# Softmax by products of ones on TensorE for batches 4 to 7, and other zero products ahead of the first chain

## The chip, the cores and the metric

The kernel runs on one core of one Trainium2 chip. The core has a matrix engine (TensorE, PE in the profile, its weight loads PEld), three engines for elementwise work (VectorE DVE, ScalarE ACT, GpSimd POOL), a queue engine (SyncE, SP), 16 DMA engines, an on-chip memory of 128 partitions and a matmul memory (PSUM) of eight banks. The metric is the device time in microseconds of one execution.

## The reference

Two parts stand behind each other. The first is a linear attention over 32 memory slots, for 8 batches, 8 heads, 576 tokens and a head size of 64; the second is a bilinear feed-forward layer over all 4608 tokens.

```python
a = np.exp(phi - max over tokens); a = a / (sum over tokens + 1e-9)
k_m = einsum('bhsm,bhsd->bhmd', a, k)
v_m = einsum('bhsm,bhsd->bhmd', a, v)
scores = q @ k_m^T / 8                       # 576 x 32 for each head
attn = softmax(scores, over the 32 slots)
x = (attn @ v_m), heads side by side         # 4608 x 512
out = ((x @ w_a) * (x @ w_b)) @ w_out        # d_ff is 1536
```

## The kernel before

Everything is done batch by batch, in 16-bit floats with 32-bit sums. The kernel never forms `attn @ v_m`: it folds the 32 memory values of each head into the weights (`fold`, tile `pva`, copied to `vab` by `take_fold`), so that the two wide products of a batch are `attn` against two folded weights of 256 x 1536.

The work of one batch is cut into named units, made by `units(b)`:

- `exp0 exp1`: exponentials of `phi` on ScalarE (L194). `qt0` to `qt3`: transposes of `q` on VectorE (L203).
- `kv`: sums of keys and values over tokens on TensorE (tile `pkv`, L212); `km` scales them on VectorE (tile `rep`). Then `rep` is transposed, either by TensorE and a VectorE copy (`kvt`, L241 and L242) or by a DMA transpose on SP's queue (`kvd`, L247).
- `sc`, or `s0` and `s1`: scores on TensorE for two groups of heads (tile `pscore`, four banks, L297). `e0`, `e1`: their exponentials on ScalarE (tile `E`, L310).
- the softmax division in one of two ways. One way: `den` multiplies `E` by a block matrix of ones on TensorE, so that each partition gets the sum of its head (tile `pD`, two products of 288 columns for each group, L320), and ScalarE takes the logarithm (`L`, L321); `nr` takes the exponential of the negated logarithm on ScalarE (`R`, L329) and multiplies `E` by it (`A`, L331), on VectorE for batches 0 to 2 and on GpSimd for batch 3. The other way, for batches 4 to 7: `ed` turns `E` by a DMA transpose so that tokens lie on partitions (L335), `sm0`, `sm1` sum 32 neighbours and take reciprocals on VectorE (L344, L345), `tn0` (GpSimd) and `tn1` (VectorE) multiply (L350), and `ad` turns the result back by another DMA transpose into `A` (L355).
- `v0 v1 v2`: folds of 512 columns each of both weights (16 products `pva`); `x0a` to `x2b` copy them out, one group on ScalarE and one on VectorE. For batches above 3 both groups of the middle fold (`x1`) are copied by ScalarE.

The wide products are `up_half` (L632): for a batch, one of 12 slices of d_ff and one half of the tokens, two products `pa` and two `pb`; ScalarE copies `pa` to `a_sb` (L640), VectorE multiplies it with `pb` into `ht` (L643). The last layer (`two_downs`, L504, tiles `py pv px`) takes two blocks of 128 tokens at a time with seven products where eight would be usual, over sums of `ht` that GpSimd forms (`sum_tokens`, tile `h_sums`, L486, four additions for a pair of blocks); sums of `w_out` are formed once by GpSimd (`sum_weights`). The first four blocks go through a plain product (`early_downs`, tile `po`, L429).

The order is written out by hand. Batches 0 and 1 start by `chain(...)`: a list of units, with `fN` for N zero products (`fill`, L151: 128 columns against a tile of zeros) and `yN` for N steps of `early_downs`. From batch 1 on, `ups(...)` runs the half steps of batch b, and after each one `work.advance()` hands out products of the last layer at a planned rate and then one entry (a slot) of the list for batch b+1 is called: `+` joins units in a slot, `'` names a unit of the batch after, `_` one of the batch before, `dN` pulls N products of the last layer, `L` calls `load` for two batches ahead, `-` is empty. Entries left over run behind the last half step. `second` serves batch 2 (units of 3 and 4), `every` batches 3 to 5, `last` batch 6. `work.settle()` ahead of scores and folds of later batches pulls products until a bank is given back. Eight PSUM banks are handed out in rotation by `banks`; a bank taken with `hold` stays out of it until it is freed.

Each engine works its own instructions in the order in which they were issued and waits where data or a buffer is not ready. `load(b)` issues four transfers on GpSimd's queue, behind whatever GpSimd was given before.

Of the kernel before, what the change touches and what calls it, by code (L numbers as in the profile page):

```python
# [18 lines left out]
def kernel(  # L19
# [127 lines left out]
    def fill(n, cols=512):  # L147

        pw = banks.tile([P, 512], F32, name="pw")
        for _ in range(n):  # L150
            nc.tensor.matmul(pw[:, :cols], warm[:, :P], warm[:, :cols], start=True, stop=True)  # L151

# [33 lines left out]
    def units(b):  # L186
# [136 lines left out]
        def normalise(g, hfs=slice(0, 2)):  # L323
# [6 lines left out]
            engine = nc.vector if b < 3 else nc.gpsimd  # L330
            engine.tensor_tensor(out=attn[b][:, g, sl], in0=t["E"][:, g, sl], in1=t["R", g][:, sl], op=ALU.mult)  # L331

        def e_turn():
            t["ET"] = mid.tile([P, 2, S], F16, name="E").rearrange("p g s -> p (g s)").rearrange("p (n x) -> p n x", x=P)
            nc.sync.dma_start_transpose(out=t["ET"], in_=t["E"].rearrange("p g s -> p (g s)"))  # L335

        def blocks(x):
            return t["ET"][:, slice(0, 5) if x == 0 else slice(5, 9)].rearrange("p n (j m) -> p (n j) m", m=M)

        def token_sums(x):  # L340
            if x == 0:
                t["sum"] = small.tile([P, 36], F32, name="sum")
            out = t["sum"][:, slice(0, 20) if x == 0 else slice(20, 36)]
            nc.vector.tensor_reduce(out=out, in_=blocks(x), axis=mybir.AxisListType.X, op=ALU.add)  # L344
            nc.vector.reciprocal(out=out, in_=out)  # L345

        def token_normalise(x):
            sums = t["sum"][:, slice(0, 20) if x == 0 else slice(20, 36)]
            engine = (nc.gpsimd, nc.vector)[x]
            engine.tensor_tensor(out=blocks(x), in0=blocks(x), in1=sums.unsqueeze(2).to_broadcast(list(blocks(x).shape)),  # L350
                                 op=ALU.mult)

        def a_turn():
            attn[b] = mid.tile([P, 2, S], F16, name="A")
            nc.sync.dma_start_transpose(out=attn[b].rearrange("p g s -> p (g s)").rearrange("p (n x) -> p n x", x=P),  # L355
                                        in_=t["ET"].rearrange("p n x -> p (n x)"))
# [20 lines left out]
        def take_fold(lo, hi, z):  # L377
            copies = (nc.scalar.copy, nc.scalar.copy if b > 3 and lo == 512 else nc.vector.tensor_copy)
            for g, engine_copy in enumerate(copies):
                pva, bank = t["pva", lo, z][g]  # L380
                engine_copy(out=vabs[b][z][:, g, lo:hi], in_=pva[:, 0:hi - lo])  # L381
                banks.free(bank)

        def one(f, *a):
            return lambda: f(*a)
# [30 lines left out]
        u["ed"] = e_turn  # L416
        for x in range(2):
            u[f"sm{x}"] = one(token_sums, x)
            u[f"tn{x}"] = one(token_normalise, x)
        u["ad"] = a_turn  # L420
# [248 lines left out]
    def half_steps(b, hf, lo=0):  # L669

        return [(b, i, (hf,)) for i in range(lo, NFF)]
# [50 lines left out]
    fill(64, P)  # L722
    chain(0, "exp0 exp1 f18 ks0 ks1 f4 kt0 qt0 qt1 f2 kt1 f4 qt2 qt3 f2 s0 e0 f2 den00 s1 e1 f8 den10 nr00 nr10 vs0 vs1 den01 den11 nr01 f4 vt0 vt1 hv0a nr11 hx0a f6 a0.0 a1.0 hv0b hx0b a0.1 a1.1 hv1a hx1a b0 b1 a3 hv1b a2 hx1b v1a x1a b2 b3 a4 a5 v1b x1b a6 a7 b4 b5 v2a x2a b6 b7 a8 a9 L v2b x2b a10 a11 b8 b9 b11 b10")
# [4 lines left out]
    ups(half_steps(1, 0, 4), slots(1, "- v2a+x2a+v2b+x2b - qt0' qt1'+exp0' exp1'+qt2' - kv'+km'+y9"))  # L728
    work.plan(S + HALF, 10)
    ups(half_steps(1, 1, 4), slots(2, "qt3 kvt - sc+e0+e1+den0+den1+nr0 - - L v0+nr1+x0b - - d4+v1+x0a+x1a+x1b d1"))  # L730
# [39 lines left out]
```

## Time and profile before

| | |
|---|---|
| times of three runs | 241.89, 241.90, 242.19 us |
| the profiled execution | 242.19 us, its span 240.5 us |
| TensorE busy | 228.8 us, 3070 products |
| VectorE busy | 170.4 us, 416 instructions |
| ScalarE busy | 153.4 us, 394 instructions |
| GpSimd busy | 152.4 us, 129 instructions |
| moved by DMA | 37.27 MB in 38436 packets |

The span runs from the first to the last instruction of the core; the time also holds what lies around it. A row of the profile names the line of the kernel, the engine, the operation, the tiles as out<-in, shapes, and either a count with busy time, mean duration and idle time ahead of it, or a start and a duration. An arrow names the instruction that ended a wait. Products on TensorE overlap, so that the distance from one start to the next, not the duration, is what a product takes of the engine's time; that distance is called the spacing below. Bank numbers and buffer numbers are left out of names.

### The profile page before, as it was taken

How to read it: one execution, taken by the hardware profiler on the slowest of the kernel's cores; microseconds unless marked ns; L12 is line 12 of the kernel's file. 1: busy time of each engine (PE TensorE's matmuls, PEld its weight loads, DVE VectorE, ACT ScalarE, POOL GpSimd, SP SyncE). 2: the span in 40 equal slices, each digit the busy share in tenths (PEclk: the TensorE clock that was granted, in tenths of full speed). 3: DMA queues.
4: the chain of work that ended last, by engine and by line, in shares of the span. 5: the costliest groups of instructions: out<-in, count | busy, mean ns of one | idle time of the engine just before them, and what ended most of it. 6: DMA issues, size and time to landing. Idle time of an engine off the chain costs nothing.

```text
span 240.5 us, 7733 instructions
## 1 busy us (share of the span) xinstructions
PE 228.8 (95%) x3070; PEld 168.4 (70%) x3070; DVE 170.4 (71%) x416; ACT 153.4 (64%) x394; POOL 152.4 (63%) x129
## 2 busy tenths in 40 slices
PE   7868999999987999999999999999999999999993
PEld 7634664456664877868777877868777778888882
DVE  4635784469949977979786777679776776656642
ACT  2266671669696579777778458776776777465330
POOL 7953244499999419593879699692929265946001
PEclk9999999999999999999999999999999999999999
DMA  6999999999989999044599748998332332032145
GB/s 234 236 197 207 206 257 207 253 211 279 224 229 209 226 227 222 19 96 92 133 222 237 106 97 181 211 185 120 61 91 51 88 79 60 12 80 64 40 107 142
DMA packets 38436, 37.27 MB, mean 155 GB/s; under 512 B 14688, under 2 KB 32480, under 8 KB 38400
## 3 DMA queue, kind: packets, MB, share of 16 engines
q0 software_dynamic: 19264, 23.14, 52.2%
q1 hardware_dynamic: 18624, 12.85, 24.4%
q10 hardware_dynamic: 512, 0.79, 1.0%
q8 instruction: 24, 0.39, 0.6%
q14 instruction: 12, 0.10, 0.1%
HBM read 42.47 MB, written 9.44 MB: 216 GB/s over the span
## 4 chain that ended last, share of the span: by engine, by line
PE 75%; DMA 16%; DVE 2%; POOL 2%; issue 1%; ACT 1%; DVEq 0%; POOLq 0%
PE pa L632 18%; PE py L504 17%; PE pb L632 17%; PE pv L504 9%; DMA phi_sb<-in_phi_dram 6%; DMA wo_sb<-in_moe_w_out_dram 5%; PE pva L368 5%; DMA wa_sb<-in_moe_w_a_dram 5%; PE px L504 4%; PE pkv L212 2%; PE po L429 2%; PE pscore L297 1%; DVE A L331 1%; ACT E L310 1%; POOL q_sb L90 0%
## 5 line engine op out<-in xcount | busy, mean ns | idle before, releaser
L643 DVE TENSOR_TENSOR ht<-a_sb,pb 128x288 f16<-128x288 f16 x168 | 71.9, 445 | 32.0 <-ACT a_sb L640 23.9
L632 PEld LDWEIGHTS <-vab 128*128 128x128 f16 x768 | 72.4, 98 | 24.0 <-issue 5.9
L640 ACT CAST a_sb<-pa 128x288 f16<-128x288 f32 x168 | 65.5, 411 | 30.9 <-PE pa L632 29.4
L632 PE MATMUL pb<-A,vab 128*128 128x288 f16 x384 | 75.0, 286 | 0.9 <-ACT vab L381 0.5
L632 PE MATMUL pa<-A,vab 128*128 128x288 f16 x384 | 75.7, 287 | 0.1
L486 POOL TENSOR_TENSOR h_sums<-ht 128x768 f16<-128x768 f16 x28 | 46.3, 1657 | 27.2 <-DVE ht L643 27.2
L504 PEld LDWEIGHTS <-h_sums 128*128 128x128 f16 x384 | 37.2, 98 | 7.7 <-issue 1.4
L381 ACT CAST vab<-pva 128x512 f16<-128x512 f32 (+1 forms) x60 | 32.0, 574 | 9.4 <-PE pva L368 9.3
L504 PEld LDWEIGHTS <-ht 128*128 128x128 f16 x288 | 27.9, 98 | 6.0 <-issue 0.9
L381 DVE CAST vab<-pva 128x512 f16<-128x512 f32 (+1 forms) x44 | 26.8, 635 | 5.4 <-PE pva L368 5.2
L504 PE MATMUL py<-w_sums,h_sums 128*128 128x256 f16 x192 | 30.6, 273 | 0.0
L486 POOL TENSOR_TENSOR h_sums<-h_sums,ht 128x768 f16<-128x768 f16 x14 | 23.1, 1653 | 1.0
L486 POOL TENSOR_TENSOR h_sums<-ht,h_sums 128x768 f16<-128x768 f16 x14 | 23.0, 1642 | 0.9
L310 ACT ACTIVATE E<-pscore 128x288 f16<-128x288 f32 x32 | 10.9, 416 | 9.3 <-PE pscore L297 9.1
L504 PE MATMUL py<-w_sums,ht 128*128 128x256 f16 x96 | 16.1, 273 | 0.1
L511 ACT ACTIVATE u<-py 128x256 f32<-128x256 f32 x32 | 12.3, 384 | 5.6 <-PE py L504 5.1
L504 PE MATMUL pv<-w_sums,h_sums 128*128 128x256 f16 x96 | 15.9, 273 | 0.0
L504 PE MATMUL py<-wo_sb,ht 128*128 128x256 f16 x96 | 15.9, 273 | 0.0
L504 PE MATMUL px<-wo_sb,ht 128*128 128x256 f16 x96 | 15.2, 273 | 0.0
L203 DVE STREAM_TRANSPOSE qT<-q_sb 128x288 f32<-128x288 f32 x32 | 14.6, 462 | 0.0
L194 ACT ACTIVATE exp_sb<-phi_sb 128x576 f16<-128x576 f32 x16 | 10.8, 689 | 5.4 <-DMA phi_sb<-in_phi_dram 5.4
L504 PE MATMUL pv<-wo_sb,h_sums 128*128 128x256 f16 x96 | 14.2, 273 | 0.0
(69 smaller groups left out, 265.5 us busy)
## 6 DMA issues: line engine op xcount, KB each, us to landing
out_dram<-o_sb SPq DMA_DIRECT2D x68, 128.0 KB, 2.5
phi_sb<-in_phi_dram POOLq DMA_DIRECT2D x8, 576.0 KB, 5.8
kv_sb<-in_v_dram POOLq DMA_DIRECT2D x7, 576.0 KB, 11.0
kv_sb<-in_k_dram POOLq DMA_DIRECT2D x7, 576.0 KB, 8.6
q_sb<-in_q_dram POOLq DMA_DIRECT2D x6, 576.0 KB, 13.8
wo_sb<-in_moe_w_out_dram POOLq DMA_DIRECT2D x6, 256.0 KB, 13.8
q_sb<-in_q_dram POOLq DMA_DIRECT2D x4, 288.0 KB, 9.9
wa_sb<-in_moe_w_a_dram POOLq DMA_DIRECT2D x2, 512.0 KB, 13.7
```

Of the source, the lines that this page charges most:

```text
L194: nc.scalar.activation(out=t["exp"][:, 2 * z:2 * z + 2, :, :], in_=phis[b][:, 2 * z:2 * z + 2, :].rearrange("p c (i m) -> p c i m", m=M), ...
L203: nc.vector.transpose(out=t["qT"][:, hp, :].bitcast(F32), in_=qs[b][:, hp, :].bitcast(F32))
L212: nc.tensor.matmul(t["pkv"][g][0][32 * j:32 * j + 32], t["exp"][64 * r:64 * r + 64, hp, i, :], kvs[b][64 * r:64 * r + 64, :, hp, D * i:D * ...
L310: nc.scalar.activation(out=Ev[:, g, :, z, :], in_=pss, func=AF.Exp, scale=1.0 / (8.0 * CS))
L368: nc.tensor.matmul(t["pva", lo, z][g][0][32 * j:32 * j + 32, 0:hi - lo], t["kvT"][64 * r:64 * r + 64, 4 + g, M * j:M * j + M], w_sbs[z][64 ...
L381: engine_copy(out=vabs[b][z][:, g, lo:hi], in_=pva[:, 0:hi - lo])
L486: engine.tensor_tensor(out=out, in0=in0, in1=in1, op=op)
L504: nc.tensor.matmul(po, lhs[:, i], rhs[:, i], start=first and i == 0, stop=i == KH - 1, skip_group_check=not first)
L511: nc.scalar.mul(out=x, in_=po, mul=scale)
L632: nc.tensor.matmul(ps, vabs[b][x][:, g, P * i:P * (i + 1)], attn[b][:, g, HALF * hf:HALF * (hf + 1)], start=(g == 0), stop=(g == 1))
L640: nc.scalar.copy(out=a_sbs[b, i, hf], in_=ps)
L643: nc.vector.tensor_tensor(out=ht[:, i, t0:t0 + HALF], in0=a_sbs.pop((b, i, hf)), in1=ps, op=ALU.mult)
```

## The change

In front of the first chain, 64 full zero products become 46 full ones, 48 products of a 64 x 32 tile of zeros with 64 columns at four positions of the array in turn, and 14 full ones. In the first chain there are fewer zero products: 32 in place of 50.

The second way of dividing is taken out: batches 4 to 7 use `den` and `nr` like the others. `nr` multiplies on VectorE for batches 0 and 1 only and on GpSimd from batch 2. The second group of every fold is copied by VectorE again. The lists of slots for batches 2 to 7 are written anew; with them, batch 4's keys and values are transposed by TensorE (`kvt'`) in place of a DMA, `load(4)` is called ahead of batch 2's half steps, and `L` stands later in the lists.

```diff
+    def fill_tiles(n):
+        pw = banks.tile([P, 64], F32, name="pw")
+        for x in range(n):
+            j = x % 4
+            nc.tensor.matmul(pw[32 * j:32 * j + 32], warm[0:64, 0:32], warm[0:64, 0:64],
+                             start=True, stop=True, tile_position=(0, 32 * j))
...
-            engine = nc.vector if b < 3 else nc.gpsimd
+            engine = nc.vector if b < 2 else nc.gpsimd
             engine.tensor_tensor(out=attn[b][:, g, sl], in0=t["E"][:, g, sl], in1=t["R", g][:, sl], op=ALU.mult)
-        def e_turn():
-        def blocks(x):
-        def token_sums(x):
-        def token_normalise(x):
-        def a_turn():
...
-            copies = (nc.scalar.copy, nc.scalar.copy if b > 3 and lo == 512 else nc.vector.tensor_copy)
-            for g, engine_copy in enumerate(copies):
+            for g, engine_copy in enumerate((nc.scalar.copy, nc.vector.tensor_copy)):
...
-    fill(64, P)
-    chain(0, "exp0 exp1 f18 ks0 ks1 f4 kt0 qt0 qt1 f2 kt1 f4 qt2 qt3 f2 s0 e0 f2 den00 s1 e1 f8 den10 nr00 nr10 vs0 vs1 den01 den11 nr01 f4 vt0 vt1 hv0a nr11 hx0a f6 a0.0 ...")
+    fill(46, P)
+    fill_tiles(48)
+    fill(14, P)
+    chain(0, "exp0 exp1 f8 ks0 ks1 f4 kt0 qt0 qt1 f2 kt1 f2 qt2 qt3 s0 e0 den00 s1 e1 den10 nr00 nr10 f4 vs0 vs1 den01 den11 nr01 f4 vt0 vt1 hv0a nr11 hx0a f6 a0.0 ...")
...
-    ups(half_steps(1, 0, 4), slots(1, "- v2a+x2a+v2b+x2b - qt0' qt1'+exp0' exp1'+qt2' - kv'+km'+y9"))
+    ups(half_steps(1, 0, 4), slots(1, "- v2a+x2a+v2b+x2b+qt0' - - qt1'+exp0' exp1'+qt2' - kv'+km'+y9"))
     work.plan(S + HALF, 10)
-    ups(half_steps(1, 1, 4), slots(2, "qt3 kvt - sc+e0+e1+den0+den1+nr0 - - L v0+nr1+x0b - - d4+v1+x0a+x1a+x1b d1"))
-    second = "v2_+d2+x2a_+x2b_+exp0 - exp1 - kv+km+d2 qt0 d4+qt1+kvt qt2 L+d1+qt3+sc+e0 - d2+v0+e1+x0a+x0b - den0+exp0'+d2 v1+nr0+x1a x1b+d10+exp1' - qt0' v2+x2a+x2b+kv' - den1+km0' km1'+kvd' nr1+qt1' qt2' qt3' - d6"
-    every = "exp0' sc+exp1'+e0+e1+v0+x0a+x0b+d3+ed - kv'+km0' km1' - sm0 sm1+tn0+kvd' - tn1+d2 d3 v1+qt0'+x1a+ad d3+L+x1b qt1' - qt2' - v2+x2a+x2b - qt3' - - - - -"
-    last = "sc e0+e1+ed - v0+x0b - - sm0 x0a+sm1+tn0 d2+v1+d3+x1b+tn1 - ad+d6 x1a - - - - v2+x2a - - - - - x2b"
+    ups(half_steps(1, 1, 4), slots(2, "qt3 kvt - sc+e0+e1 - den0+den1+nr0 - v0+nr1+x0a x0b - v1+x1b x1a"))
+    second = "v2_+d1+x2a_+exp0 x2b_ exp1 - kv+km+d2 qt0 d4+kvt+qt1 - qt2+qt3+sc+e0 - e1+v0+d2+x0a+x0b den0+d3 exp0' v1+nr0+x1a x1b+qt0' L+d5 den1 v2+x2a exp1'+qt1'+x2b - - qt2'+kv'+nr1+km' - - qt3'+kvt'+d5"
+    every = "- sc+e0 e1 den0 nr0+v0+x0a+x0b - - exp0' exp1' - v1+x1b+x1a+kv'+km0'+d3 - den1+km1' kvd'+qt0' - - nr1+qt1' v2+x2a+x2b - qt2' - qt3' - - L"
+    last = "sc+e0 d3 - e1 v0+x0b - - den1 - - den0+d1 x0a+v1+x1b x1a+nr0 - - - v2+x2a - nr1 - - - - x2b"
     for b in range(2, B):
+        if b == 2:
+            load(4)
```

## The prediction

> **What bounds the kernel now.** I read the page first (engines, slices), then the chain of waits for the first 50 us, then TensorE's instructions in order of time with the idle time before each, and last VectorE and GpSimd around the one place where TensorE idles.
>
> ```profile
> span 240.5 us, 7733 instructions
> PE 228.8 (95%) x3070; PEld 168.4 (70%) x3070; DVE 170.4 (71%) x416; ACT 153.4 (64%) x394; POOL 152.4 (63%) x129
> PE   7868999999987999999999999999999999999993
> PEclk9999999999999999999999999999999999999999
> ```
> TensorE is the bound almost everywhere; only the first four slices, two near 70 us and the last are not full, and the granted clock is full throughout.
>
> ```profile
> 33.90 12.86 DMA wo_sb<-in_moe_w_out_dram
> ...
> 46.80 0.59 PE po L429 x2
> ```
> This is the chain of waits. Up to 46.76 us it is made of GpSimd's transfer issues and landings alone; the fifth slice of `wo_sb` then releases TensorE, which had idled 0.35 us. So what becomes faster before 46.8 us only lengthens that wait, and what becomes slower by up to 0.35 us costs nothing.
>
> ```profile
> 65.70 0.65 PE L297 MATMUL pscore<-qT,kvT 32*32 32x288 f16 x32
> 66.95 0.41 PE L320 MATMUL pD<-E,ones 128*128 128x288 f16 x2 [0.61 <-ACT E L310]
> 67.56 0.41 PE L320 MATMUL pD<-E,ones 128*128 128x288 f16 x2 [0.20 <-ACT E L310]
> ...
> 74.21 0.41 PE L368 MATMUL pva<-wb_sb,kvT 64*32 64x512 f16 x7 [1.22 <-DVE vab L381]
> 74.55 0.28 PE L504 MATMUL pv<-wo_sb,h_sums 128*128 128x256 f16 x1
> 74.67 0.44 PE L632 MATMUL pa<-A,vab 128*128 128x288 f16 x2
> ```
> ```profile
> 69.31 0.46 DVE L331 TENSOR_TENSOR A<-E,R 128x576 f16<-128x576 f16 x1 [3.09 <-ACT R L329]
> ...
> 71.36 2.19 DVE L331 TENSOR_TENSOR A<-E,R 128x576 f16<-128x576 f16 x1
> ```
> ```profile
> 71.58 1.65 POOL L486 TENSOR_TENSOR h_sums<-ht 128x768 f16<-128x768 f16 x1
> ```
> TensorE, VectorE, GpSimd in order of time: batch 2's softmax. The sums of exponentials wait for the exponentials just issued, and the second multiply takes 2.19 us instead of 0.46, ending just after a GpSimd addition ends; four `vab` copies queue behind it, and TensorE waits for them.
>
> ```profile
> 80.00:100.00 20.00, 20.00 (x357) 15.25 (x337) 16.91 (x45) 15.67 (x42) 10.72 (x9) 1.00 0.88 184
> ...
> 200.00:220.00 20.00, 20.00 (x174) 16.80 (x172) 13.35 (x31) 11.83 (x32) 13.53 (x9) 1.00 0.13 29
> ```
> Stretches of 20 us (columns: length, busy of PE, its weight loads, DVE, ACT, POOL; clock, DMA share, GB/s). TensorE shows no idle time from 80 to 220 us, so each product added there lengthens the run by its spacing, unless it fills a hidden wait.
>
> **The change part by part.** *Products of ones for batches 4 to 7 (`den`, L320), 16 more.* Spacing from
> ```profile
> 89.52 0.41 PE L320 MATMUL pD<-E,ones 128*128 128x288 f16 x2
> 89.77 0.38 PE L504 MATMUL py<-w_sums,h_sums 128*128 128x256 f16 x2
> ```
> Two take 0.245 us (89.52 to 89.77, start to start), so 8 pairs cost 1.96 us, all in the full stretch. They come one to three slots after the exponentials they read, so no wait is added.
>
> *Batch 4's key/value transposes by TensorE (`kvt`) instead of by DMA (`kvd`):* six products; the same six of batch 3 start at 82.67 and their successor at 83.00: 0.33 us, plus a VectorE copy of 0.53 us. Scores follow two slots and some 2 us later, which covers the copy.
>
> *The other engines.* ScalarE gains 16 logarithms (four in 1.35 us: 5.4) and 8 exponentials of 0.71 (5.7) and gives 8 copies of 0.60 to VectorE (-4.8). VectorE loses the reductions (5.9), reciprocals (2.1) and multiplies (3.1) of the token path and batch 2's two multiplies (2.65), and gains those 8 copies at 0.68 (5.5). GpSimd loses four multiplies of 1.26 and gains ten of 1.28: +7.7, to 160 of 240 us. SP loses nine DMA transposes, so its stores go out earlier or at the same time. All this is worth nothing while TensorE covers it; the gaps before GpSimd's additions (1.7 to 4.8 us after 110 us, all for data) are the room. Without that cover, each late multiply costs what it is late.
>
> *Transfers moved (`load(4)` to `load(7)`).* GpSimd runs ahead of TensorE, so a load starts when the instruction before it on GpSimd ends, not at its slot. `load(4)` now stands behind batch 2's multiplies: from 68.6 to about 73 us; its phi is first read some 15 us later and lands 4.9 us after issue; values land 10 to 13 us after a load's start. `load(7)` starts some 4 us before batch 5's products, and by the spacings of the products ahead its values are needed 12 us after those begin. Zero, with 3 us to spare.
>
> *Batch 2's softmax:* sums of exponentials now stand two slots behind the scores, and the multiplies are on GpSimd. Walking it with the rows' spacings (copies 0.36, logarithms 0.34, R 0.71, `vab` copies 0.5 and 0.62, A 1.28): exponentials done 67.5, two copies 68.2, logarithms 69.5, R 70.1, GpSimd's A 71.4 (its additions ended at 68.6); second R 71.75, A 73.1. The fold (`v0`, `v1`) waits for banks at 70.4 and 72.2, so batch 2's first product ends about 73.2. Before it ended at 74.9, but with three more products of 0.109 already done: the gain is 1.7 - 0.33 = 1.4 us. Bounds: nothing, if A is late by 1.4 us, to 2.0, the idle time of the three rows above. I take 1.4.
> The Trainium skill, SBUF — State Buffer, "Who interferes with whom", says a VectorE operation with two SBUF inputs and a GpSimd one exclude each other for the whole instruction. That fits the 2.19 us. By that rule, each of the ten multiplies added on GpSimd can block a VectorE operation of that kind for 1.28 us; if all ten struck the path, an estimate by that page would make the sum 12.8 us worse. After the change hardly an operation of that kind is left on VectorE between 80 and 220 us, and no row here shows `ht` (one input in PSUM) blocked.
>
> *The burst at the scores of batches 4 to 6.* Now the scores, both phi exponentials, four score exponentials, fold and copies share one slot. After it 16 `pva` products need 0.89 us (104.50, 129.23 and 157.52 in the chain) where the others need 0.56. Spread over slots 1 to 4, that wait goes: 3 x 0.33 = 1.0 us.
>
> *New waits.* Nothing here prices them: lower bound 0; upper, as many as the old schedule had, one burst wait of 0.33 for each of the five batches 3 to 7, 1.65. I know two candidates: batch 4's `kv'+km'` late in batch 2 puts 2.3 us on VectorE in one slot (0.2 us), and batch 5's fold runs 12 products in a row whose first partial sum leaves ScalarE late (0.15 us). I take 0.6, nearer to these.
>
> *The front: 60 full zero products instead of 82 ahead of the first real one, and 48 tiled ones; 18 fewer behind.* TensorE waits at 8.72 us for exponentials of phi in any case. Full ones start 12 a us at first (0.083 apart) and some 20 a us when fast (0.05): 46 x 0.083 + 22 x 0.05 = 4.9 us from 1.26. The 48 tiled ones lie between 0.5 us (`pk`, 64x64 in tiles: 72 from 15.03 to 15.73 us) and 48 x 0.083 = 4.0. So the front ends between 6.7 and 10.2 us: in time, or 1.4 late, of which 0.35 is covered (+1.1). I take the tiled row, the nearest in shape: in time, zero. Fewer zero products behind it can only bring TensorE earlier to the 46.76 us landing.
> The Trainium skill, TensorE: Matmul & The Clock Gate, "Wait — 56ns, not 53.3ns?", gives a floor of 25 ns from start to start: 1.2 us for the 48. The `pk` row, at 10 ns, contradicts it; by both the front ends before 8.72 and the sum stays.
>
> Sum: +1.96 + 0.33 - 1.4 - 1.0 + 0.6 = +0.5 us. The profiled execution took 242.19 us (span 240.5, 1.7 around it), the slowest of three and 0.3 above the median. On it this gives 242.7; on the median 241.9 it gives **242.4**.
>
> **The rivals.** *Faster.* Batch 2 yields the whole 2.0 us of idle time and the new waits stay at zero: 2.29 - 2.0 - 1.0 = -0.7, 241.2. For it: the three idle rows end for reasons that the new order takes away. Against: my walk still finds two bank waits in that fold. It decides from 1.8 us at batch 2 with no new wait elsewhere. 0.18.
> *GpSimd late.* The multiplies stand behind additions of 1.65 us. Batch 7's second one has, by my count, additions of 6.6 us and another multiply ahead after mid-batch 6 and ends 9.6 us after it; TensorE needs it at 10.4 (12 steps of 0.49 and 36 of 0.109, a fold of 0.56). Two or three such misses of 0.5 us: +1.0 to 1.5 more, 243.4 to 243.9. Against: 63% busy and waiting for data. 0.2.
> *The clock.* With a thinner front the tensor clock could stay or fall back to the first microseconds' spacing (0.083 against 0.05). Some 4 us of products between 8.7 and 18 us would take half as long again or more: +2 less 0.35, 244.0. For it: TensorE may idle 2 us before 8.72; the longest idle time after its start is now 1.22. Against: granted clock full even with a quarter idle at 10 to 15 us. 0.07.
> *The early saving counts after all,* if that landing moves: at most the 0.35 us. Inside the range.
>
> **How the numbers follow.** The forecast has 0.55, by itself 241.9 to 242.9. About 0.2% (0.48 us, what a measurement of this kernel can tell from no change) parts it: half of it is slower. Slower 0.28 + 0.2 + 0.07 = 0.55; same 0.25; faster 0.18 + 0.02 = 0.2. The range leaves out half of the faster case below and the clock and the worst of GpSimd above: 241.2 to 243.6.
>
> **What would show it.** Busy TensorE products of ones: 32 at the same spacing; full stretches from 80 to 220 us without idle time; batch 2's first product about 1.7 us earlier and no 2.19 us multiply; `pva` 16 in about 0.6 us in batches 4 to 6; the wait for `wo_sb` ending near 46.8 and longer than 0.35. Wrong if TensorE idles for A or `h_sums`, if the wait for `wo_sb` ends elsewhere, or if the first chain's products run at the slow spacing.

## The result and the profile after

The changed kernel takes 257.76 us (median of four runs, 257.09 to 258.16) against 241.89 (241.63 to 242.19): ratio 1.065, 95% interval 1.063 to 1.068. The forecast of 242.4 us missed by 15 us. The profiled execution took 257.09 us, its span is 255.4 us. First the page of the changed kernel:

```profile
span 255.4 us, 7812 instructions
PE 232.8 (91%) x3116; PEld 170.4 (67%) x3116; DVE 178.7 (70%) x403; ACT 159.1 (62%) x410; POOL 159.3 (62%) x135
PE   8779999602999999999999999999999999999993
PEclk9977999965799999999999999999999999999999
```

Slice 9 of TensorE's row (51 to 57 us; a slice is 6.4 us) is empty and the two beside it are partly so, and the granted clock, which was full throughout before, is low in two places: in slices 3 and 4 (13 to 26 us), and again in the hole and just behind it. TensorE's waits, the longest first (total, times, longest):

```profile
PE pa L609 <- DVE vab L363: 13.0, 1, 13.0
PE pD L328 <- ACT E L318: 1.6, 2, 0.8
```

One single wait holds 13.0 us. The chain of waits (start, duration, what) says what is behind it:

```profile
47.40 0.69 ACT R L337
48.09 0.02 issue
48.11 13.66 DVE A L339
61.77 0.35 DVE vab L363
62.12 0.05 issue
62.16 0.90 PE pa L609 x3
```

It is `A`, the second softmax multiply of batch 1 on VectorE, an operation that the change does not touch. It lasts 13.66 us; in the kernel before the same row, on VectorE in order of time, is

```profile
47.17 0.46 DVE L331 TENSOR_TENSOR A<-E,R 128x576 f16<-128x576 f16 x1 [0.36 <-ACT R L329]
```

What GpSimd does meanwhile, in order of time, in the changed kernel:

```profile
47.94 0.74 POOL L90 DMA_DIRECT2D q_sb<-in_q_dram  x1
48.70 3.23 POOL L448 TENSOR_TENSOR w_sums<-wo_sb 128x768 f16<-128x768 f16 x2
51.88 3.21 POOL L448 TENSOR_TENSOR w_sums<-wo_sb,w_sums 128x768 f16<-128x768 f16 x2
55.06 3.21 POOL L448 TENSOR_TENSOR w_sums<-wo_sb 128x768 f16<-128x768 f16 x2
58.24 3.21 POOL L448 TENSOR_TENSOR w_sums<-wo_sb,w_sums 128x768 f16<-128x768 f16 x2
```

and in the kernel before:

```profile
48.43 0.74 POOL L90 DMA_DIRECT2D q_sb<-in_q_dram  x1 [0.40 <-DVE vab L381]
49.19 3.24 POOL L471 TENSOR_TENSOR w_sums<-wo_sb 128x768 f16<-128x768 f16 x2
```

These are the eight additions of `sum_weights`, behind the issue of the last transfer of `load(3)`. They end at 61.45 us, `A` at 61.77. Before, `A` was done at 47.63 us, 0.8 us ahead of that issue; now it starts at 48.11, 0.17 us behind the issue's beginning. The two have moved towards each other: `A` starts 0.94 us later, and the first addition 0.49 us earlier (48.70 in place of 49.19). Where `A`'s lateness begins is seen in TensorE's clock, in stretches of 2 us (length, busy of PE, weight loads, DVE, ACT and POOL, clock, DMA share, GB/s) of the changed kernel:

```profile
12.00:14.00 2.00, 0.84 (x22) 0.33 (x18) 0.51 (x2) 1.44 (x5) 1.35 (x2) 1.00 1.35 199
14.00:16.00 2.00, 1.59 (x79) 1.26 (x79) 0.47 (x2) 1.44 (x5) 1.01 (x2) 0.83 1.47 202
16.00:18.00 2.00, 1.39 (x22) 0.72 (x19) 1.32 (x7) 1.37 (x4) 1.14 (x2) 0.50 1.44 192
18.00:20.00 2.00, 2.00 (x26) 1.20 (x18) 0.42 (x1) 0.83 (x3) 0.93 (x2) 0.50 1.27 207
```

The clock falls to one half after a stretch in which TensorE was busy for 0.84 of 2 us (before: 1.43 of 2, and full clock). The first chain then runs later: the `pb` products of batch 0 that wait for a copy of `vab` start at 25.16 us in place of 24.12.

The full stretches further on, of the changed kernel (15 us later than before for the same work):

```profile
80.00:100.00 20.00, 19.68 (x317) 14.10 (x316) 15.56 (x38) 15.49 (x41) 15.98 (x13) 1.00 0.69 139
...
200.00:220.00 20.00, 20.00 (x195) 15.82 (x193) 13.54 (x30) 15.45 (x41) 11.75 (x8) 1.00 0.25 54
```

Between 80 and 120 us TensorE idles 0.4 us in all, and from 120 to 240 us not at all: what the softmax part moved has opened no hole of any size.

So my theory after the result has three links. *The front lets the clock fall; the first chain is late by about a microsecond; `A` then comes to its turn when GpSimd has begun a run of additions, and is shut out until the last of them.* The earlier start of the additions is not explained by it. Its rivals: the lateness alone is harmless and the low clock or something else makes the stall; the softmax part costs the time; the zero products matter by their kind, or only by their amount.

### The profile page after: what moved, and what is told of

Its sections match the earlier page's. It is cut to its first block, busy times and chain, and to the rows that moved or that the text cites. A ratio compares the mean times of both kernels' runs of the same rounds, so it can differ in the third digit from the quotient of the medians.

```text
span 255.4 us, 7812 instructions
## 1 busy us (share of the span) xinstructions
PE 232.8 (91%) x3116; PEld 170.4 (67%) x3116; DVE 178.7 (70%) x403; ACT 159.1 (62%) x410; POOL 159.3 (62%) x135
## 4 chain that ended last, share of the span: by engine, by line
PE 83%; DVE 8%; ACT 4%; DMA 2%; issue 1%; DVEq 0%; POOLq 0%
PE pa L609 19%; PE pb L609 18%; PE py L481 17%; PE pv L481 8%; DVE A L339 5%; PE pva L351 5%; PE px L481 4%; PE po L406 4%; DMA phi_sb<-in_phi_dram 2%; PE pkv L220 2%; PE pscore L305 2%; PE pk L268 2%; PE pD L328 1%; ACT L L329 1%; ACT E L318 1%
## 5 line engine op out<-in xcount | busy, mean ns | idle before, releaser
L620 DVE TENSOR_TENSOR ht<-a_sb,pb 128x288 f16<-128x288 f16 x168 | 73.2, 449 | 38.3 <-ACT a_sb L617 28.5
L609 PEld LDWEIGHTS <-vab 128*128 128x128 f16 x768 | 73.3, 99 | 38.9 <-DVE vab L363 13.7
L617 ACT CAST a_sb<-pa 128x288 f16<-128x288 f32 x168 | 67.0, 408 | 39.5 <-PE pa L609 38.3
L609 PE MATMUL pa<-A,vab 128*128 128x288 f16 x384 | 77.7, 293 | 13.0 <-DVE vab L363 13.0
L363 DVE CAST vab<-pva 128x512 f16<-128x512 f32 (+1 forms) x52 | 32.3, 643 | 6.9 <-PE pva L351 6.4
L363 ACT CAST vab<-pva 128x512 f16<-128x512 f32 (+1 forms) x52 | 27.7, 571 | 8.8 <-PE pva L351 8.2
L339 DVE TENSOR_TENSOR A<-E,R 128x288 f16<-128x288 f16 (+1 forms) x6 | 15.3, 2556 | 4.9 <-ACT R L337 4.8
L339 POOL TENSOR_TENSOR A<-E,R 128x576 f16<-128x576 f16 x12 | 15.3, 1275 | 4.3 <-ACT R L337 4.3
L481 PE MATMUL py<-wo_sb,ht 128*128 128x256 f16 x96 | 16.7, 273 | 0.0
L329 ACT ACTIVATE L<-pD 128x288 f32<-128x288 f32 x32 | 11.6, 426 | 5.1 <-PE pD L328 4.9
## 6 DMA issues: line engine op xcount, KB each, us to landing
wo_sb<-in_moe_w_out_dram POOLq DMA_DIRECT2D x6, 256.0 KB, 13.7
```

Of the source, the lines that this page charges most:

```text
L329: nc.scalar.activation(out=t["L", g][:, sl], in_=pD, func=AF.Ln)
L481: nc.tensor.matmul(po, lhs[:, i], rhs[:, i], start=first and i == 0, stop=i == KH - 1, skip_group_check=not first)
L609: nc.tensor.matmul(ps, vabs[b][x][:, g, P * i:P * (i + 1)], attn[b][:, g, HALF * hf:HALF * (hf + 1)], start=(g == 0), stop=(g == 1))
L617: nc.scalar.copy(out=a_sbs[b, i, hf], in_=ps)
L620: nc.vector.tensor_tensor(out=ht[:, i, t0:t0 + HALF], in0=a_sbs.pop((b, i, hf)), in1=ps, op=ALU.mult)
```

## The experiments

Each kernel is compared with runs of the kernel before on its own chip; the chips differ between groups of runs. Three single executions of kernels with the old fills, two of the kernel before and one of e1, took 257.3 to 258.7 us at a mean clock of 0.96; the ratios leave them out.

### Which part: e1 to e4

e1 takes the changed kernel and gives it the zero products of before:

```diff
-    fill(46, P)
-    fill_tiles(48)
-    fill(14, P)
-    chain(0, "exp0 exp1 f8 ks0 ... f2 kt1 f2 qt2 qt3 s0 e0 den00 s1 e1 den10 nr00 ...")
+    fill(64, P)
+    chain(0, "exp0 exp1 f18 ks0 ... f2 kt1 f4 qt2 qt3 f2 s0 e0 f2 den00 s1 e1 f8 den10 nr00 ...")
```

> The changed kernel with the zero products of before (64 in front, the first chain's list of before); softmax, lists of slots and copies stay as changed. Theory A: the loss is one VectorE multiply of batch 1 (A, 0.46 us before, 13.66 us after) that reaches its turn 0.9 us later, behind GpSimd's transfer issue and eight additions; it is late only because the tensor clock fell to half between 15 and 23 us, and that comes from the zero products. Then the clock stays full here, that multiply takes 0.46 us again, and the time is 241 to 243 us. Rival B: the new softmax and lists themselves make the collision or the loss; then the time stays above 250 us. The prediction's own sum for this part alone is +0.5 us (242.4).

Measured: 241.45 us, ratio 0.9975 (0.996 to 0.999). The stall goes with the zero products (one of the ten executions had it all the same, by its time), and the rest of the change makes the kernel faster by 0.25%. e1's `A` on VectorE and the issue on GpSimd:

```profile
47.60 0.46 DVE L339 TENSOR_TENSOR A<-E,R 128x576 f16<-128x576 f16 x1 [0.37 <-ACT R L337]
```

```profile
47.95 0.74 POOL L90 DMA_DIRECT2D q_sb<-in_q_dram  x1 [0.69 <-DMA wo_sb<-in_moe_w_out_dram]
```

Here `A` starts 0.35 us ahead of the issue and is done 0.64 us ahead of the additions, which begin at 48.70 us as in the changed kernel. So their earlier start does not come from the zero products. The distance between being in time and a stall is some tenths of a microsecond.

e2 does the reverse: the kernel before with the new zero products alone.

> The kernel before with the new zero products alone (46 full, 48 tiled, 14 full in front, the first chain's new list). Theory A: clock at half for some us near 15 to 23 us, batch 1's second VectorE multiply over 10 us, time 254 to 257 us. Rival B: the clock may dip, but the time stays at 242 to 243 us, since a dip alone costs about 1 us less 0.35.

Measured once: 242.15 us, clock 0.63 from 14 to 16 us and 0.50 from 16 to 20, and no stall: `A` starts at 47.72 and takes 0.46, the issue comes at 48.20. So the new fills bring the fall of the clock, and need not bring the stall.

e3 (old front with `f18`, thin chain) and e4 (new front with `f8`, the chain's old zero products) split the fills:

> The changed kernel with the front of before (64 and 18 full zero products, none tiled), the rest of the first chain's list as changed (14 fewer zero products behind the first sums). If the missing products inside the chain let the clock fall, it still falls near 15 us and the time is 256 to 258 us. If the tiled products in front do it, the clock stays full and the time is 241 to 243 us.

> The changed kernel with its new front (46, 48 tiled, 14 and 8), and inside the first chain behind that the zero products of before (f4 f2 f4 f2 f2 f8 f4 f4 f6). If the missing products inside the chain let the clock fall, the clock stays full here and the time is 241 to 243 us; if the tiled front does it, the clock falls and the time is 256 to 258 us.

Measured once each: e3 241.47 us, clock full from 10 to 26 us; e4 257.81 us, clock 0.50 from 14 to 22 us and `A` of 12.92 us from 49.58. By these two runs the front does it and not the thin chain; ten runs of the same split (e10a, e10b) say otherwise below.

### Kind or amount, and lateness without a low clock: e5, e6

```diff
 e5, on the changed kernel            e6, on e1
-    fill(46, P)                      -    chain(0, "... a10 a11 b8 b9 b11 b10")
-    fill_tiles(48)                   +    chain(0, "... a10 a11 b8 b9 b11 b10 f24")
-    fill(14, P)
+    fill(69, P)
```

> The changed kernel with its 48 tiled zero products replaced by 9 whole ones (128 by 128), which take the same half microsecond, so that the front is 69 whole products and the first chain keeps its thin list. Theory (the kind of product counts: a stretch of tiled products lets the granted clock fall): clock near 1.0 from 8 us on, batch 1's second multiply takes 0.46 us, 241.3 to 241.9 us. Rival (the amount counts: the front is shorter than before by some 13 products and the chain thinner): clock 0.5 between 14 and 22 us as in the changed kernel, the multiply late and held for 13 us, 257 to 258 us.

Measured once: 257.66 us, clock 0.50 from 14 to 22 us, `A` 12.98 us from 48.87. That was for the amount; ten runs of the same front (e10c) look different, below.

> The changed kernel with the fills of before, and 24 more whole zero products at the end of the first chain: a lateness of about 1.3 us without a fall of the clock. Theory (late is enough: the multiply that comes after GpSimd's last transfer issue is held through the eight additions): the multiply starts near 48.9 and takes 12 to 13.5 us, TensorE idles some 12 us, 254.5 to 257.5 us. Rival (the low clock, or something else in the tiled front, makes the stall): the multiply takes 0.5 to 3.5 us, 242.5 to 245.5 us.

Measured once: 257.78 us, with the clock at 1.00 in every stretch from 6 to 50 us. VectorE:

```profile
48.14 13.48 DVE L339 TENSOR_TENSOR A<-E,R 128x576 f16<-128x576 f16 x1 [0.36 <-ACT R L337]
```

Lateness is enough. The low clock is one way to be late and not part of the stall (behind the stall it falls too, 0.56 from 50 to 60 us, since TensorE stands).

### Take the additions out of the way: e7, and put gaps between them: e7b, e11

e7 makes the eight additions wait for `A`, by a copy of one column, which the first addition overwrites:

```diff
     load(3)
+    nc.gpsimd.tensor_copy(out=w_sums[:, 0, 0, 0:1], in_=attn[1][:, 1, S - 1:S])
     sum_weights()
```

> The changed kernel as it is, with one GpSimd copy of a single column of batch 1's attention in front of the eight additions, so that the additions wait until the multiply is done. Theory (the additions hold the multiply): it still starts late, near 48.1, waits at most for the transfer issue on GpSimd to end and is done by 49.3; the additions begin after it; what is left is the first chain's lateness of about 1 us and the part of it that other waits take up, 241.6 to 243.2 us. Rival (the multiply is held by something that the additions only accompany): 255 to 258 us, and the additions 13 us late.

Measured: 243.56 us (243.43 to 243.84), ratio 1.007 (1.005 to 1.009), on a clock of 0.979 in every run. `A` is even later than in the changed kernel and takes its 0.46 us; the additions begin at 50.42:

```profile
49.62 0.46 DVE L339 TENSOR_TENSOR A<-E,R 128x576 f16<-128x576 f16 x1 [0.36 <-ACT R L337]
```

One ordering on GpSimd takes away 14 of the 16 us. What remains is the price of the low clock, more than the 241.6 to 243.2 that I expected.

e7b leaves the guard out and changes the order of the eight additions, so that some of them wait on GpSimd for the one just before (four, not the five that my expectation says):

```diff
-        for out, in0, in1 in ((t[0], ...), (t[1], ... t[0]), (t[2], ...), (t[3], ... t[1])):
-            for x in range(2):
+        for x in range(2):
+            for out, in0, in1 in ((t[0], ...), (t[1], ... t[0]), (t[3], ... t[1]), (t[2], ...)):
```

> The changed kernel with the eight additions in another order, so that five of them in place of none need the result of the addition just before and wait for it on GpSimd. Theory (the multiply is shut out because the additions follow each other without a gap): it gets in at the first such gap, after one or two additions, takes 2 to 7 us, 244 to 250 us. Rival (a gap of some tens of ns isn't enough, all eight go first): it takes 13 us again, 257 to 258 us.

Measured once: 241.69 us, but nothing is told by it: in that run `A` started at 47.66, 0.08 us ahead of the issue, and met no addition. So e11 repeats it on e6, which is late without a fall of the clock:

> The late kernel without a fall of the clock (24 whole products at the end of the first chain), with the eight additions in an order in which four of them, the second first, need the addition just before and wait for it on GpSimd. Theory (VectorE is shut out only as long as the additions follow without a gap): the multiply begins near 48.1 as before but gets in at a gap behind the first or second addition, 2 to 5 us, 244 to 247.5 us. Rival (such a gap isn't enough): 12 to 13.5 us again, 257 to 258.5 us.

Measured: eight runs, five of 241.82 to 241.94 us and three of 244.10 to 245.44; the profiled one (244.19) is of the second kind; what `A` did in the five short ones is not on record. Its VectorE and GpSimd:

```profile
48.14 2.46 DVE L339 TENSOR_TENSOR A<-E,R 128x576 f16<-128x576 f16 x1 [0.36 <-ACT R L337]
```

```profile
48.63 1.65 POOL L448 TENSOR_TENSOR w_sums<-wo_sb 128x768 f16<-128x768 f16 x1
50.36 3.46 POOL L448 TENSOR_TENSOR w_sums<-wo_sb,w_sums 128x768 f16<-128x768 f16 x2
```

`A` came at the same time as in e6, 48.14, and ended at 50.60 in place of 61.62. The first addition ends at 50.28, the second starts at 50.36: a gap of 0.08 us is where VectorE got in. In e6 and in the changed kernel the next addition starts 1.6 us after the last one with no gap in the rows, and none of seven such seams let it in. The gap is not made by `A`: e7b has the same 0.08 us (50.15 to 50.23) with no multiply waiting. The multiply of batch 2 in the kernel before agrees: it too ended (73.55) behind one addition (73.23), which a gap of 0.08 us follows. That is the mechanism, shown by one edit that leaves the amount of work and the lateness alone, in one profile of each order.

e15, the late kernel with the guard, asks whether the transfer issue holds VectorE as well:

> The same late kernel with the additions in their old order and the guard copy in front of them. The multiply then meets the issue of the last transfer alone. Theory (the issue holds it too, to its end): it takes 0.5 to 1.2 us where it begins inside the issue, and ends behind the issue; the additions begin after it; 242.4 to 243.4 us. Rival (the issue does not hold it): 0.46 us although the issue runs; 242.3 to 242.9 us. Both say that the 13 us are gone.

Measured: 242.04 us (241.81 to 243.45, nine runs), ratio 1.001 (1.000 to 1.002); the 13 us are gone again. Its batch 1 `A` does not answer the question: it came at 49.52, after the issue had ended at 49.40. Rows of the first chain do; in the kernel before, VectorE and GpSimd:

```profile
17.17 0.31 DVE L331 TENSOR_TENSOR A<-E,R 128x288 f16<-128x288 f16 x1 [0.24 <-ACT R L329]
```

```profile
17.06 0.71 POOL L104 DMA_DIRECT2D wo_sb<-in_moe_w_out_dram  x1 [0.67 <-DMA wb_sb<-in_moe_w_b_dram]
```

A multiply of half the columns runs wholly inside a transfer issue and takes 0.31 us, as long as in e2 with no issue beside it (17.06 to 17.37). So an issue alone does not hold it. In the changed kernel `A` would then have been done at 48.57, 0.13 us ahead of the first addition's recorded start; what held it for these 0.13 us is not shown.

### The price of the front, read with the guard: e9, e10, e12, e13

With the guard no kernel can fall into the stall, so the zero products can be priced. All of these are the changed kernel with the guard; only the zero products differ (`f18` and `f8` are those between the front and the first sums):

| | front | chain | us, median (lowest to highest, runs) | ratio to before | mean clock |
|---|---|---|---|---|---|
| e9 | 64, `f18` | old | 241.26 (241.13 to 241.88, 6) | 0.998 (0.996 to 0.999) | 0.986 to 1.000 |
| e10a | 64, `f18` | thin | 241.72 (241.01 to 242.84, 10) | 0.999 (0.998 to 1.001) | 0.979 to 1.000 |
| e10b | 46 + 48 tiled + 14, `f8` | old | 242.45 (241.32 to 243.53, 10) | 1.002 (1.000 to 1.004) | 0.979 to 1.000 |
| e10c | 69, `f8` | thin | 241.47 (241.28 to 241.61, 10) | 0.998 (0.997 to 0.999) | 0.985 to 1.000 |
| e12 | 46 + 48 tiled + 18, `f18` | old | 243.89 (243.52 to 244.46, 4) | 1.009 (1.007 to 1.011) | 0.977 to 0.991 |
| e13 | 60, `f8` | thin | 241.64 (241.41 to 243.30, 10) | 1.001 (0.999 to 1.003) | 0.979 to 1.000 |
| e7 again | 46 + 48 tiled + 14, `f8` | thin | 242.16 (241.61 to 243.84, 10) | 1.003 (1.001 to 1.006) | 0.979 to 0.993 |

e9 and the three e10 ran together, as did e12, e13 and e7 again.

> The changed kernel with the fills of before (front and first chain) and the guard copy on GpSimd that lets the eight additions begin only after batch 1's second multiply. Theory (the rare time of 258 us in the run with the old fills alone is the same stall): 241.3 to 241.8 us in every run, clock 0.98 or more. Rival (the rare long run has another cause): one run in five to ten near 258 us again. If the guard itself costs something, it is at most its 0.2 us on GpSimd, and nothing on the path.

> The changed kernel with the guard and with the front of before (64 whole products, then 18 behind the first sums), but the thin list of zero products in the rest of the first chain. With the guard the cost of the clock is read alone. Theory (the front makes the clock fall, not the thin chain): clock 0.995 or more and 241.4 to 241.9 us. Rival (the thin chain does it): clock about 0.979 and 243.2 to 244.0 us, as with the guard alone.

> The changed kernel with the guard and with the new front (46 whole, 48 tiled, 14 whole, then 8 behind the first sums), but the zero products of before in the rest of the first chain. Theory (the front makes the clock fall): clock 0.975 to 0.985 and 243 to 244.5 us. Rival (the thin chain does it): clock 0.995 or more and 241.4 to 241.9 us.

> The changed kernel with the guard, the 48 tiled products replaced by 9 whole ones of the same total length, and the thin chain. Theory (the length of the front counts, not the kind of product in it: the one run of this kind without the guard had the clock at one half): clock about 0.979 and 243.2 to 244.0 us in most runs. Rival (the tiled kind counts, and that run was one of the rare ones): clock 0.995 or more and 241.4 to 241.9 us.

> Fills of before, with the guard, and the 48 tiled products on top of the 64 whole ones in the front, so that the front is longer than before and nothing is taken out. Theory (the tiled products themselves bring it: 48 more instructions for 0.5 us of work, and TensorE then stands with no wait shown, as issue, in the first scores near 11 to 12.7 us): the first sixteen scores take 0.95 to 2 us in place of 0.76 to 0.80, the clock falls near 14 us, 242 to 243.6 us. Rival (only the thinner front counts): scores 0.76 to 0.80, clock 0.995 or more, 241.1 to 241.6 us.

> The changed kernel with the guard and without the 48 tiled products, nothing in their place: 60 whole products, then the thin chain. Theory (the tiled products bring the stand in the scores and with it the fall of the clock): scores 0.76 to 0.80, 241.3 to 241.9 us. Rival (the length of the front counts): the clock falls at least as far as with the tiled products, 242.5 to 244 us.

> The changed kernel with the guard alone once more, beside the two variants of its front on the same chip. Clock 0.978 to 0.992 with 242.3 to 243.7 us if the tiled products bring the fall; the same as the variant without them, within 0.3 us, if they do not matter.

What follows. e9: all six runs lie below the median of the kernel before beside them (241.91), none near 258 us, as the theory had it; six are few for that, and since the rare long executions were not profiled, that they are the same stall is inferred from their time and clock alone. e12 against e9, which differ in the 48 tiled products alone: all four runs with them take 243.5 us or more, all six without them 241.9 or less (on two chips; 1.1% apart by their ratios). e10c against both runs of e7: whole products of the same total length keep all ten runs at or below 241.61, by the ratios 0.5% and 0.9% faster than the tiled ones. So it is the kind, in the main, and my conclusion from e5's single run went too far: that front, too, lets the clock fall in some executions, and in e5's this led to the stall.

e10a, the old front with the thin chain, undoes what I read from e3. Six of its ten runs have a mean clock of 0.979 to 0.986, where I expected 0.995 or more. The same kernel but for the guard kept the full clock in e3; e10a's profile did not. Stretches of 2 us, first of e3, then of e10a:

```profile
12.00:14.00 2.00, 0.80 (x29) 0.33 (x18) 0.56 (x2) 1.47 (x5) 1.31 (x2) 1.00 1.35 199
14.00:16.00 2.00, 1.61 (x83) 1.39 (x82) 0.50 (x2) 1.54 (x6) 0.97 (x2) 1.00 1.45 196
```

```profile
12.00:14.00 2.00, 0.66 (x17) 0.23 (x17) 0.26 (x1) 1.63 (x5) 1.36 (x2) 1.00 1.34 198
14.00:16.00 2.00, 1.92 (x82) 1.55 (x82) 0.80 (x4) 1.39 (x5) 1.04 (x2) 0.78 1.45 195
16.00:18.00 2.00, 1.39 (x23) 0.68 (x21) 1.07 (x7) 1.20 (x5) 1.10 (x2) 0.50 1.46 198
```

So the thin chain alone can let the clock fall as well, though its ratio of 0.999 cannot be told from e9's. Nor does the new front always do it: e10b, where I expected 243 us or more, has a median of 242.45, and two of its ten runs kept the full clock. Even the old zero products do not shut a fall out: of the 85 executions of the kernel before without a stall that ran beside the experiments, 11 have a mean clock of 0.984 or 0.985, the others 0.996 or more, while none of the fourteen of e7 is above 0.993. What the zero products decide is how often the clock falls and how far.

In e12 TensorE stands; its waits in the first 30 us that are put down to nothing are

```profile
PE pw L151 <- issue: 1.4, 1, 1.4
PE pT L286 <- issue: 0.6, 1, 0.6
```

and in e10b:

```profile
PE pscore L305 <- issue: 1.0, 1, 1.0
```

Behind a tiled front TensorE stands with no wait that the profile names, in e10b for 1.0 us in the first scores, in e12 for 0.6 in the transposes before them and for 1.4 up to 18.1 us. The 48 tiled products take 96 instructions (each with its weight load) for half a microsecond; that later instructions are then not there in time would explain it, but no row shows it. In the changed kernel the first sixteen scores take 1.15 us, in the kernels with whole fronts 0.76 to 0.80; but e7 again's profile shows 0.80 behind a tiled front, so the stand is not in every execution. Nor do stands come behind tiled products alone, or a fall behind every stand: with the old zero products the kernel before has one of 0.7 us ahead of 14.7 and e1 one of 0.9 ahead of 15.2, both with the clock full, and e15 one of 1.1 ahead of 14.7, with the clock at 0.75 from 14 to 16 us and 0.50 behind. In e12 the clock is full up to 18 us and falls to 0.53 right behind the second stand.

The pair on one chip that differs in the tiled products alone, e13 and e7 again, does not part them by its intervals. The amount has some weight too: without the tiled products (e13) three runs of ten still came out at 243.0 to 243.3, as four of ten at 243.3 to 243.8 with them (e7 again). How far the clock falls differs between executions of one kernel. The Trainium skill, TensorE: Matmul & The Clock Gate, "What's actually happening", says that the clock follows how busy TensorE has lately been, judged over windows of some 3.4 us, and calls an idle window what throttles it. In the changed kernel it fell with no idle time above 0.81 us between the first product and the fall, so less than an idle window can be enough. How little is not shown: 0.84 us busy of 2 came ahead of the fall there, 0.80 (e3) and 0.85 (e10c) came ahead of none. The section adds that these windows run free of the kernel's start. The profiles fit that. A stretch of 2 us with mean clock c holds 4 x (1 - c) us at one half, so the low clock lasted 0.28 + 2.00 + 1.12 = 3.4 us in e13 (clocks 0.93, 0.50, 0.72), 0.68 + 6.00 + 0.16 = 6.8 in the changed kernel (0.83, three times 0.50, 0.96) and 1.00 + 8.00 + 1.24 = 10.2 in e4 (0.75, four times 0.50, 0.69): one, two and three times 3.4. The low stretches of the other nine profiles that have one ahead of any stall are of these three lengths too; the twelve begin at times from 13.0 to 18.1 us. That the spread of the times from 241.6 to 243.8 comes from it is not shown.

### Batch 2 by itself: e8

The kernel before with the edits for batches 2 and 3 alone (batch 2's multiplies on GpSimd, `second` and the lists ahead of it, `load(4)`), batches 4 to 7 still by DMA transposes:

```diff
-            engine = nc.vector if b < 3 else nc.gpsimd
+            engine = nc.vector if b < 2 else nc.gpsimd
...
-    ups(half_steps(1, 1, 4), slots(2, "qt3 kvt - sc+e0+e1+den0+den1+nr0 - - L ..."))
+    ups(half_steps(1, 1, 4), slots(2, "qt3 kvt - sc+e0+e1 - den0+den1+nr0 - v0+nr1+x0a x0b - v1+x1b x1a"))
```

> The kernel before with the part of the change for batches 2 and 3 alone: batch 2's multiply on GpSimd, the new lists of the preparation of batches 2 and 3 (which prepare batch 4's keys by products in place of a transfer), load of batch 4 where the change has it; batches 4 to 7 keep the softmax by transfers. Theory (the softmax stage of batch 2 gains 1.8 us, and the products for the denominators of batches 4 to 7 give back the rest): 239.9 to 240.8 us. Rival (the gain needs the rest of the change, since it is taken back in the burst at the scores of batch 4): 241.4 to 242.2 us.

Measured: 241.96 us (240.90 to 242.42, ten runs), ratio 1.000 (0.9985 to 1.0013): the rival's number. From score to score the profiles say where the time goes (start of a batch's scores to the next, us; the products in a stage are counted from the instruction lists):

| stage | before | e8 | e9 | what differs in e9's products |
|---|---|---|---|---|
| batch 2 to 3 | 20.23 | 18.33 | 18.34 | nothing |
| 3 to 4 | 18.09 | 18.19 | 18.19 | +6 transposes, -6 `px` |
| 4 to 5 | 24.74 | 25.81 | 25.33 | +4 `pD`, +6 `px` (e8: `px` only) |
| 5 to 6 | 28.29 | 28.29 | 28.34 | +4 `pD`, -1 `py` |
| 6 to 7 | 23.80 | 23.80 | 23.97 | +4 `pD`, +1 `py` |
| 7 to the end | 59.65 | 59.59 | 59.96 | +4 `pD` |

Batch 2's stage gains 1.9 us with the same products in it (e1 and the changed kernel have 18.34 as well, e2, with the old lists, 20.21). e8's profile gives 1.07 back between the scores of batches 4 and 5: 6 `px` at 0.109 are 0.65 of it, and the old burst is still there (its second eight `pva` take 0.80). That leaves e8's profile 0.9 us ahead. The median of its runs shows nothing of this: the profiled execution lies 0.7 us under e8's median, that of before 0.3 us over its own. Why is not shown. In e9, where the multiplies of batch 2 are on GpSimd, TensorE and then GpSimd read, in order of time,

```profile
65.27 0.71 PE L305 MATMUL pscore<-qT,kvT 32*32 32x288 f16 x32
...
67.24 0.96 PE L328 MATMUL pD<-E,ones 128*128 128x288 f16 x4
...
72.07 0.53 PE L609 MATMUL pa<-A,vab 128*128 128x288 f16 x2
```

```profile
69.54 1.28 POOL L339 TENSOR_TENSOR A<-E,R 128x576 f16<-128x576 f16 x1 [1.24 <-ACT R L337]
70.99 1.28 POOL L339 TENSOR_TENSOR A<-E,R 128x576 f16<-128x576 f16 x1 [0.17 <-ACT R L337]
```

None of the three idle times of before shows ahead of batch 2's first wide product, which starts 6.80 us after the scores in place of 8.97.

## Why the prediction was wrong, and where it was right

**"What becomes slower by up to 0.35 us costs nothing"** is the step that failed. The wait for `wo_sb` covers lateness on TensorE. It says nothing of `A`, which is worked at 47.17 us, 0.4 us after that wait, and had a deadline of its own: GpSimd's additions, at 49.19 in the kernel before and at 48.70 in the changed one. That the additions would move was not in the prediction either. I read GpSimd and VectorE only around batch 2, where the same thing had cost 1.7 us, and for the stretch from 80 to 220 us. The row at 71.36 (2.19 us, ending just after an addition) was the warning; the place to hold against it was every other two-input multiply left on VectorE, of which batch 1's stood 1.5 us ahead of eight additions in a row. I also priced a collision at one GpSimd instruction (1.28 us). The Trainium skill, SBUF — State Buffer, "Who interferes with whom", calls the ports that VectorE and GpSimd share an exclusive lock and says, of VectorE's two-port modes, that whoever issues first has them for the whole instruction. e6 and e11 show more than one instruction for a multiply of two on-chip inputs; it is held until GpSimd pauses: 13.48 us over eight additions without a gap, 2.46 us where a gap of 0.08 us follows the first.

**The front "in time, zero".** The length was right: the tiled products took 0.5 us as taken from the `pk` row, and the first sums started at 8.44 us against 8.72. The counts were off: ahead of the first sums stand 68 whole zero products in place of 82 (the sum uses 68, the text says 60), behind them 22 in place of 32, so 10 fewer and not 18; the first chain has 30 of its own, not 32. What failed is that I asked of the front and the chain only when they end, and not in what state they leave TensorE. In the kernel before it was busy for no more than 1.1 to 1.4 of every 2 us from 12 to 18 us, with the old number of zero products; that was there to be read.

**The rival of the clock** had the right mechanism and nearly the right place (8.7 to 18 us foreseen, 15 to 22 measured). Its price by itself, +2 less 0.35, is borne out with the guard: e7 lies 0.5% and, on the other occasion, 0.9% above e9 by their ratios to before, 1.3 to 2.2 us. Two things failed: its chance of 0.07, argued from the old front's full clock, and that it ended at its own price, where it was the trigger for the 13 us. The sum of the loss from the profiles of e1 and the changed kernel: `A` ends 13.7 us later (48.06 to 61.77), the scores of batch 2 start 15.4 us later (65.66 to 81.09), with the clock at 0.50 again for 4 us behind the stall, and the end is 15.6 us later.

**The softmax part, forecast +0.5 us, is -0.6 (e9: ratio 0.9977 of 241.9; interval -0.9 to -0.3).** Term by term, from the table of stages. Products of ones: 16, and 0.49 us for four by the spacing that I took; the count is as forecast. Batch 2: 1.9 us in place of 1.4, near the upper bound of 2.0; and the three products that I subtracted are not missing, since the stage has the same products as before. Burst: the four stages from batch 4's scores on are 1.12 us longer in e9, while their extra products come to 1.96 + 6 x 0.109 = 2.61; so 1.5 us went where I took 1.0. New waits: in the stage of batch 3, 0.10 + 0.65 - 0.33 = 0.4, where I took 0.6 over all. So the sign turned on three sizes of 0.2 to 0.5 us, all on the same side. *GpSimd late* did not happen: e9 shows TensorE waiting for no late multiply, though GpSimd has ten of these more.

**The signs named beforehand** were good ones. "The first chain's products run at the slow spacing" and "TensorE idles for A" are both what the trace shows, only for batch 1's `A` and not for the moved ones. The wait for `wo_sb`, expected to grow, is gone: the products that waited until 46.80 us start at 47.33 in the changed kernel. In e9 they start at 46.41, without a wait, so the landing can move, as the last rival supposed.

## What to carry to other kernels

Before an edit that moves the start by tenths of a microsecond is priced at nothing, look for the neighbours that pass each other closely: here a VectorE operation with two on-chip inputs and a long run of GpSimd work, whose order in time was left to chance. Make such an order explicit with a dependency (here a copy of one column, 0.2 us on GpSimd), or leave gaps in the run; then the kernel's time no longer hangs on it, and the parts of a change can be measured by themselves. The changed kernel with the old zero products and this guard, 241.26 us, has the lowest median here, faster than before by 0.1 to 0.35%.

## What the runs showed of the hardware

- A VectorE multiply of two 16-bit inputs (0.46 us) took 13.66 us beside eight GpSimd additions that follow each other directly (changed kernel), and 2.46 us where the second of them began 0.08 us after the first one's end (e11). A transfer issue on GpSimd did not hold one (0.31 us inside an issue, kernel before).
- 48 products of a 64 x 32 tile with 64 columns passed in 0.5 us, 10 ns each (0.75 us in e7's profile), but fronts that hold them left TensorE standing 1.0 us (e10b) and 2.0 us (e12) without a named cause, and cost 1.3 us (e7 again) to 2.6 us (e12) against e9 by their ratios to before.
- The granted clock, where it fell ahead of a stall, stayed at one half for 3.4, 6.8 or 10.2 us in all twelve profiles, although TensorE was then busy nearly all the time (changed kernel, 18 to 20 us: 2.00 of 2). Stretches in which TensorE was busy for 0.66 to 0.85 of 2 us were followed by a fall in some executions and not in others (e10a, e3).
